# Attention and feed-forward on one core: the last unit's output in three PSUM places, and an order planned with another measure of TensorE's load

## The chip, the cores and the metric

The kernel runs on one core of one Trainium2 chip. The metric is the device time of one execution in microseconds (us); lower is better. The time before is the median of three runs. A profiled execution of the same kernel, taken apart from those three, gives the rows that are read here; its own time and its span stand in the table below. A difference of 0.3% is about what a measurement of this kernel can tell from none.

## What is computed

```python
# q, k, v: (4 batches, 8 heads, 768, 64); centroids (8, 16, 64); w_in (512, 2048); w_out (2048, 512)
q_assign = argmax(q_n @ c_n.T); k_assign = argmax(k_n @ c_n.T)      # nearest of 16 centroids, per head
mask = q_assign[:, :, :, None] == k_assign[:, :, None, :]
scores = where(mask, q @ k.T / sqrt(64), -1e9)
attn = exp(scores - max); attn = attn / (attn.sum(-1) + 1e-9)
x = (attn @ v).transpose(0, 2, 1, 3).reshape(3072, 512)
h = x @ w_in
g = where(h >= 1, h, where(h <= -1, 0, (h + 1)**2 / 4))
out = g @ w_out                                                       # (3072, 512) float32
```

All data are float32.

## The kernel before

**Tiling.** The work is cut into 12 units: four batches times three chunks of 256 queries (`u = b * NCH + c`). A unit goes through four head pairs, and each head pair through four tiles of 128 queries by 768 keys (`at_scores`, `at_soft`, `at_av`), and then through eight feed-forward steps `f` of 256 hidden columns (`ffn1`, `ffn2`). Float32 operands are split into two float16 parts, so that a product is three matmuls. Unit 0 is an exception: its operands are not split yet, and it works with float32 matmuls and turns the attention tiles with TensorE (`by_tensor`), where later units turn them by DMA.

**One tile of unit 0.** TensorE makes the scores (matmuls with 64 rows of the array in use, into `pair0` or `pair1`), VectorE reduces them (`tensor_tensor_reduce`, shown as CUSTOM_DVE_ANT_0 in the profile and as ISA in the order; it writes `sS`), ScalarE takes the exponential of `sS` in place, TensorE turns `sS` in six 128x128 pieces with the identity `idf`, and ScalarE copies them out to `pT`. After four tiles `at_av_first` multiplies `pT` with `v` into `bank_a`. Unit 0 has 16 such tiles, two in flight. Beside this, VectorE and ScalarE prepare the weights (`w_bits`: three passes of VectorE over 128x1024 numbers for each of 16 blocks, in `wk` and `w`), TensorE sums each block (`w_sum`, the product `wk,ones`), and the splits of `k` and `v` are made (`n<-kv,sc`, `kv<-kv,sv`).

**PSUM.** There are eight banks: `pair[0]` and `pair[1]` (two each, L562), `bank_a`, and `bankh`, `banki`, `bankj` (L563). Scores go to `pair0` after the first units, attention products to `bank_a`, hidden layers to the last three. `ffn2` (L1343) sums a unit's output, two tiles of 128x512, in `pair[1]`: at the first step it takes the place, at the last step ScalarE copies each tile with the factor `io` to the buffer `o`, and SyncE's queue sends it to memory.

**The last step of the last unit** differs by the flag `end`: the twelve products come tile by tile, one group for each tile, there are two copies by ScalarE, and two DMAs of 256 KB.

**What sets the order.** No instruction is issued where it is written. `Recorder` (L78) records all, and `issue` (L341) plans the order of every engine with a model of the chip: `price` (L126) gives each operation a cost, `Machine` (L358) follows engines, PSUM banks, the DMA queue and TensorE's clock, `forward` picks the next instruction by priority, and `backward` makes priorities from the plan just made. That is done `BASE` times; then each seed in `NUDGES` shifts the priorities of some recorded steps a little (`nudge`, L327), and a last `forward` gives the order that is written out. Products within one `with rec.group()` stay together.

**The clock in the model.** `Machine.product` (L404) cuts time in windows of `WINDOW` ns. In each it adds up the time in which TensorE works. If that is over `SLOW` of the window (`FULL`, when the clock was low), the next window is at full clock, and otherwise at half.

Of the kernel before, what the change touches and what calls it, by code (L numbers as in the profile page):

```python
# [35 lines left out]
WINDOW, SLOW, FULL = 3413.0, 0.41, 0.77  # L36
# [12 lines left out]
BASE = 5  # L49
NUDGES = (  # L50
# [27 lines left out]
class Recorder:  # L78
# [47 lines left out]
    def price(self, eng, op, out, ins, kw):  # L126
# [13 lines left out]
        if eng == "tensor":  # L140
            n = self.free(ins[1])
            half = self.free(ins[0]) <= 64 and n > 100
            if ins[1].dtype == F32:
                turn = kw.get("is_transpose", False)
                return 109 if turn else max(n / 1.2 + 2.5, 107) if half else max(n / 0.6 + 3, 222)

            return n / 4.8 + 3 if half else max(n / 2.4 + 2.5, 24)
# [25 lines left out]
    def add(self, eng, op, fn, args, kw):  # L173
# [10 lines left out]
        assert node.eng == eng  # L184
        p = self.price(eng, op, outs[0], ins, kw)
        if isinstance(p, tuple):
            node.cost += p[0]
            node.dma = p[1:]
        else:
            node.cost += p  # L190
# [167 lines left out]
class Machine:  # L358
# [20 lines left out]
    def run(self, x, t):  # L379
# [13 lines left out]
        else:  # L393
            x.busy = self.product(t, x.cost) if e == "tensor" else t + x.cost
# [9 lines left out]
    def product(self, t, cost):  # L404

        while True:
# [5 lines left out]
            t, self.work, cost = t + part, self.work + part, cost - part / pace  # L412
# [4 lines left out]
class Node:  # L417
    def __init__(self, eng, step, i):
        self.eng, self.step, self.i, self.ev = eng, step, i, 0
        self.banks = set()  # L420
        self.turn = False
        self.cost, self.dma, self.calls, self.preds, self.succs = 0.0, None, [], {}, []
# [52 lines left out]
def tile_clustered_attention_moe(  # L475
# [867 lines left out]
    def ffn2(u, f):  # L1343
# [4 lines left out]
        g = F.pop((u, f))  # L1348
        if e["first"]:
            F[u] = view(pair[1], [CT, DM], F32)  # L1350
        po = F[u]
        terms = [(s, i, *x) for s in range(2) for i, x in enumerate(((0, 0), (0, 1), (1, 0)))]
        end = u == NU - 1 and f == NF - 1

        parts = [(terms, [t]) for t in range(CT)] if end else [(terms[:3], range(CT)), (terms[3:], range(CT))]
        for part, ts in parts:
            with rec.group():
                for s, i, ga, wa in part:
                    for t in ts:
# [19 lines left out]
        if f == NF - 1:  # L1379
            to = out.rearrange("(b p t) e -> b p t e", b=B, t=T)[b, :, c * CT : (c + 1) * CT, :]  # L1380
            for part in [slice(t, t + 1) for t in range(CT)] if end else [slice(0, CT)]:
                rec.sync.dma_start(to[:, part], ob[:, part])


# [117 lines left out]
```

## Time and profile before

| what | us |
|---|---|
| median of 3 runs (lowest, highest) | 848.51 (847.31, 849.62) |
| the profiled execution's own time | 849.15 |
| its span, first to last instruction | 847.4 |
| TensorE busy in the span | 835.1 |
| VectorE, ScalarE, GpSimd busy | 624.5, 643.4, 445.4 |
| mean granted TensorE clock | 0.997 |

The profiled execution took 1.75 us more than its span (849.15 less 847.4) and 0.64 us more than the median. In the rows, PE is TensorE's matmuls, PEld its weight loads, DVE VectorE, ACT ScalarE, POOL GpSimd and SP SyncE, whose queue issues all DMAs. A row of the timeline has the start, the length, the engine, the operation, the tiles (written <- read) and the count; in brackets stands the idle time of the engine ahead of it and what ended it. Almost every instruction is issued from one line of the recorder (L355), so that rows are told apart by tiles. PEclk is the TensorE clock that was granted, as a share of the full one.

### The profile page before, as it was taken

What the parts mean: (1) busy time and instruction counts of PE and PEld (TensorE: products, weight loads), DVE (VectorE), ACT (ScalarE), POOL (GpSimd) and SP (SyncE); (2) the same over time, 40 slices, a digit from 0 to 9 for tenths busy, and PEclk for the clock granted to TensorE, in tenths of its full rate; (3) what the DMA queues carried; (4) which work ended last, traced back from release to release, by engine and by line L of the source; (5) the groups of instructions that cost most, each with busy time, mean ns of one, the idle gap of its engine ahead of it and who ended that gap; (6) DMA issues with size and microseconds to landing.
All of it is one profiled execution on the core that took longest, in us unless ns stands there. A gap on an engine that the chain in (4) does not pass through costs nothing.

```text
span 847.4 us, 22063 instructions
## 1 busy us (share of the span) xinstructions
PE 835.1 (99%) x8767; PEld 595.1 (70%) x8767; DVE 624.5 (74%) x1405; ACT 643.4 (76%) x1129; POOL 445.4 (53%) x365
## 2 busy tenths in 40 slices
PE   8998999999999999999999999999999999999997
PEld 6765667676777777776777677776777777777764
DVE  4999999899988767677878767678877767545222
ACT  5899867899979789687777887787778687766222
POOL 2001464456657567466555666565666656555221
PEclk9999999999999999999999999999999999999999
DMA  9929998999999879799999879898999887566100
GB/s 330 322 90 216 197 239 172 197 173 197 188 180 191 154 152 180 162 182 188 196 166 193 160 154 179 158 200 177 184 184 170 144 163 129 111 124 104 20 26 25
DMA packets 405415, 141.46 MB, mean 167 GB/s; under 512 B 373952, under 2 KB 397504, under 8 KB 405312
## 3 DMA queue, kind: packets, MB, share of 16 engines
q1 hardware_dynamic: 405312, 140.05, 82.6%
q8 instruction: 68, 1.11, 0.5%
q14 instruction: 35, 0.29, 0.1%
HBM read 40.40 MB, written 6.29 MB: 55 GB/s over the span
## 4 chain that ended last, share of the span: by engine, by line
PE 90%; DVE 6%; issue 1%; ACT 1%; DMA 1%; POOL 0%; SPq 0%; ACTq 0%; DVEq 0%
PE pair L355 45%; PE banka L355 12%; PE bankj L355 11%; PE banki L355 11%; PE bankh L355 11%; DVE w L355 1%; DVE sS L355 1%; DMA q<-in_q_dram 1%; ACT sS L355 1%; DVE bankj L355 0%; DVE r L355 0%; DVE wk L355 0%; DVE n L355 0%; DVE kv L355 0%; DVE banki L355 0%
## 5 line engine op out<-in xcount | busy, mean ns | idle before, releaser
L355 POOL TENSOR_TENSOR hl<-sS,hl 128x768 f16<-128x768 f32 x176 | 297.9, 1697 | 170.4 <-ACT hl L355 123.3
L355 PE MATMUL pair<-w,g 128*128 128x512 f16 (+1 forms) x1120 | 279.3, 391 | 0.0
L355 ACT ACTIVATE sS<-sS,sbi 128x768 f32<-128x768 f32 x192 | 179.1, 933 | 81.4 <-DVE sbi L355 69.4
L355 DVE CUSTOM_DVE_ANT_0 sS<-pair,zero,er 128x768 f32<-128x768 f32 x192 | 194.1, 1012 | 51.3 <-PE pair L355 42.1
L355 PEld LDWEIGHTS <-w 128*128 128x128 f16 x1848 | 179.3, 98 | 33.5 <-issue 0.9
L355 PEld LDWEIGHTS <-g 128*128 128x128 f16 x1056 | 101.9, 98 | 102.0
L355 PE MATMUL pair<-kv,q 128*128 128x384 f16 (+1 forms) x768 | 167.8, 341 | 0.4 <-DVE sbi L355 0.4
L355 ACT CAST hl<-sS 128x768 f16<-128x768 f32 x176 | 144.8, 826 | 12.3 <-DMA pT<-hl 10.0
L355 POOL TENSOR_TENSOR g<-r,g 128x512 f16<-128x512 f32 x80 | 95.0, 1188 | 90.3 <-ACT g L355 81.1
L355 PEld LDWEIGHTS <-q 128*128 128x128 f16 x1056 | 75.9, 97 | 43.9 <-issue 4.8
L355 PEld LDWEIGHTS <-pT 128*128 128x128 f16 x3168 | 98.3, 98 | 6.2 <-issue 1.1
L355 PE MATMUL banka<-kv,pT 128*128 128x64 f16 x3168 | 99.6, 193 | 0.0
L355 ACT ACTIVATE r<-r,f_ra,f_rs 128x512 f32<-128x512 f32 x80 | 64.7, 809 | 35.8 <-DVE r L355 35.3
L355 ACT CAST g<-r 128x512 f16<-128x512 f32 x80 | 48.8, 610 | 14.2 <-DVE r L355 9.6
L355 PE MATMUL bankj<-x,w 128*128 128x256 f16 (+1 forms) x368 | 47.8, 282 | 0.1
L355 POOL TENSOR_TENSOR qn<-qn,phi 128x256 f16<-128x256 f16 x44 | 29.4, 690 | 31.2 <-DVE phi L355 22.6
L355 PE MATMUL bankh<-x,w 128*128 128x256 f16 (+1 forms) x320 | 42.4, 284 | 0.4 <-DVE r L355 0.4
L355 PE MATMUL banki<-x,w 128*128 128x256 f16 (+1 forms) x280 | 41.2, 298 | 0.0
L355 ACT ACTIVATION_READ_ACCUMULATOR sS<-sS,sbi 128x1 f32 x192 | 36.0, 188 | 0.0
L355 POOL CAST rr<-rs 128x4 f16<-128x4 f32 x4 | 1.9, 471 | 60.8 <-DVE rs L355 43.8
L355 DVE TENSOR_SCALAR r<-banki,f_lo,f_hi 128x512 f32<-128x512 f32 x27 | 21.8, 806 | 15.7 <-PE banki L355 10.5
L355 DVE TENSOR_TENSOR rb<-banka,rs 128x256 f32<-128x256 f32 x44 | 18.5, 420 | 19.9 <-PE banka L355 19.5
(267 smaller groups left out, 1143.3 us busy)
## 6 DMA issues: line engine op xcount, KB each, us to landing
w<-in_moe_w_out_dram SPq DMA_DIRECT2D x14, 512.0 KB, 5.4
kv<-in_k_dram SPq DMA_DIRECT2D x16, 384.0 KB, 4.6
q<-in_q_dram SPq DMA_DIRECT2D x12, 512.0 KB, 5.1
kv<-in_v_dram SPq DMA_DIRECT2D x16, 384.0 KB, 4.3
out_dram<-o SPq DMA_DIRECT2D x11, 512.0 KB, 3.6
w<-in_moe_w_in_dram SPq DMA_DIRECT2D x10, 512.0 KB, 8.9
word<-in_moe_w_in_dram SPq DMA_DIRECT2D x6, 512.0 KB, 5.3
o<-in_v_dram SPq DMA_DIRECT2D x8, 384.0 KB, 4.6
```

Source lines behind the costliest of these rows:

```text
L355: fn(*args, **kw)
```

## The change

It has two parts.

**The last unit.** `ffn2` hands the last unit to a new function, `ffn2_last`. It sums the output in three places: tile 0 in `pair0` (512 columns), the left half of tile 1 in `pair1` and its right half in `bank_a` (256 columns each). In steps 0 to 6 the three places stand side by side in each group; in the last step each place has a group of its own, one after the other. Then ScalarE copies place 0, VectorE place 1, and place 2 is copied by ScalarE (128 columns) and VectorE (128 columns). Two DMAs of 256 KB follow, one for each tile. For a step of the last unit there are 18 matmuls in place of 12: six of 512 columns become twelve of 256.

**The planner.** A new number, `load`, is kept for each recorded step: the time in which columns stream through the array, without the fixed time of each instruction, and counted half where the products use 64 rows or fewer. `Machine.product` adds up this load in place of the time at work. The limits are 0.367 and 0.7 in place of 0.41 and 0.77, `BASE` is 4 in place of 5, and there are 153 new seeds in place of 116.

```diff
-WINDOW, SLOW, FULL = 3413.0, 0.41, 0.77
+WINDOW, SLOW, FULL = 3413.3, 0.367, 0.7
...
-BASE = 5
+BASE = 4
 NUDGES = (
-    1942955373, 816938251, 357356202, 374281491, 1996901420, 1807131614, 1896407074, 546410407, 980899077,
...
+    2072586604, 595665893, 1371912370, 1242582630, 2050099710, 1720864319, 412320839, 382347784, 317351908,
...
-                return 109 if turn else max(n / 1.2 + 2.5, 107) if half else max(n / 0.6 + 3, 222)
+                ns = 109 if turn else max(n / 1.2 + 2.5, 107) if half else max(n / 0.6 + 3, 222)
+                self.open.load += min(ns, n / (1.2 if half or turn else 0.6)) * (1 if ins[1].shape[0] > 64 else 0.5)
+                return ns
+            self.open.load += n / (4.8 if half else 2.4) * (1 if ins[1].shape[0] > 64 else 0.5)
...
-            x.busy = self.product(t, x.cost) if e == "tensor" else t + x.cost
+            x.busy = self.product(t, x.cost, x.load / x.cost) if e == "tensor" else t + x.cost
...
-            t, self.work, cost = t + part, self.work + part, cost - part / pace
+            t, self.work, cost = t + part, self.work + part * load, cost - part / pace
...
+        if u == NU - 1:
+            return ffn2_last(f, g, e)
...
+    def ffn2_last(f, g, e):
+
+        q = DM // 2
+        places = ((0, 0, pair[0][:, :DM]), (1, 0, pair[1][:, :q]), (1, q, bank_a[:, :q]))
+        terms = [(s, i, *x) for s in range(2) for i, x in enumerate(((0, 0), (0, 1), (1, 0)))]
+        for part, ps in [(terms, [x]) for x in places] if e["last"] else [(terms[:3], places), (terms[3:], places)]:
+            with rec.group():
+                for s, i, ga, wa in part:
+                    for t, c0, po in ps:
+                        rec.tensor.matmul(
+                            po, g[:, ga, s * CQ + t * P : s * CQ + (t + 1) * P],
+                            w2[f][:, wa, s, c0 : c0 + po.shape[1]],
+                            start=(e["first"] and s == 0 and i == 0), stop=(e["last"] and s == 1 and i == 2),
+                        )
...
+        rec.scalar.activation(out=ob[:, 0], in_=p0, func=AF.Copy, scale=e["io"])
+        rec.sync.dma_start(to[:, 0], ob[:, 0])
+        rec.vector.tensor_scalar(out=ob[:, 1, :q], in0=p1, scalar1=e["io"], scalar2=None, op0=ALU.mult)
+        rec.scalar.activation(out=ob[:, 1, q : q + P], in_=p2[:, :P], func=AF.Copy, scale=e["io"])
+        rec.vector.tensor_scalar(out=ob[:, 1, q + P :], in0=p2[:, P:], scalar1=e["io"], scalar2=None, op0=ALU.mult)
+        rec.sync.dma_start(to[:, 1], ob[:, 1])
```

**Where the rows move: the turns of unit 0.** The first place is TensorE's order at the fourth head pair of unit 0 (`kv_64`; the third is `kv_63`). `pair_82` and `pair_83` are `pair0` and `pair1`, `sS_88` to `sS_90` the three buffers of reduced scores, `hl_80` and `hl_81` the 0/1 labels, `banka` is `bank_a`. Before, the turns of the last two tiles stand right behind the scores of these tiles:

```order
L355 LDWEIGHTS hl_80
L355 MATMUL pair_83<-hl_81,hl_80 128x384
L355 MATMUL pair_82<-idf,sS_88 128x128 x6
L355 MATMUL pair_83<-idf,sS_89 128x128 x6
L355 LDWEIGHTS q_66
```

Now the third head pair's product with `v` (24 matmuls, of which the last two are shown) stands ahead of these turns:

```order
L366 MATMUL banka<-pT_146,kv_63 64x256
L366 MATMUL banka<-pT_147,kv_63 64x256
L366 MATMUL pair_82<-idf,sS_88 128x128 x6
L366 MATMUL pair_83<-idf,sS_89 128x128 x6
L366 LDWEIGHTS ones
```

What moved is the product with `v`: before, it stood two tiles earlier, between the scores and the turns of the first two tiles of that head pair. There TensorE's order now has nothing between the two:

```order
L366 LDWEIGHTS hl_80
L366 MATMUL pair_83<-hl_81,hl_80 128x384
L366 MATMUL pair_82<-idf,sS_89 128x128 x6
L366 LDWEIGHTS ones
L366 MATMUL banki<-wk_69,ones 128x128
```

A sum of weights (`wk,ones`, eight matmuls) now parts the two turns there.

**VectorE ahead of the third reduction of that head pair.** `w_72` and `word_71` are raw and prepared weights, `sS_88,sbi_137` is the reduction of the third tile. Before, between the reductions of the second and the third tile:

```order
L355 SCALAR_TENSOR_TENSOR w_72<-w_72 128x1024
L355 TENSOR_REDUCE zm_134<-bankj 128x16
L355 TENSOR_SCALAR wk_69<-wk_69 128x1024
L355 SCALAR_TENSOR_TENSOR kv_62<-kv_62,sv_168 128x768
L355 SCALAR_TENSOR_TENSOR w_72<-w_72,wk_69 128x1024
L355 RECIPROCAL sc_158<-ik_153 128x1
L355 TENSOR_TENSOR er_133<-bankj,zm_134 128x16
L355 SCALAR_TENSOR_TENSOR w_72<-w_72 128x1024
L355 ISA sS_88,sbi_137<-pair_82,zero,er_132 128x768
```

Now:

```order
L366 TENSOR_TENSOR zs_131<-banki,mx_129 128x256
L366 SCALAR_TENSOR_TENSOR w_72<-w_72,wk_69 128x1024
L366 TENSOR_SCALAR qn_67<-zs_131 128x16x16
L366 SCALAR_TENSOR_TENSOR w_72<-w_72 128x1024
L366 TENSOR_TENSOR bankj<-zs_131,has_130 128x256
L366 SCALAR_TENSOR_TENSOR w_72<-word_71 128x1024
L366 ISA sS_88,sbi_137<-pair_82,zero,er_132 128x768
```

Three passes over weights stand there in both; one is of another block now, and the split of `kv_62` has moved ahead of the first tile's reduction.

**The end of the program.** The second part of the change is seen on ScalarE and VectorE, with the engines that each instruction waits for (`g_77` is the last step's g, `o_68` the output buffer, `hl_79` the last step's hidden layer). ScalarE before:

```order
L355 CAST g_76<-hl_81 128x512 [waits DVE_49,PE_49,Pool_49]
L355 ACTIVATE hl_79<-hl_79,f_ra_185,f_rs_188 128x512 [waits DVE_49]
L355 CAST g_77<-hl_79 128x512 [waits DVE_49,PE_49,Pool_49]
L355 ACTIVATE o_68<-pair_83,f_io_182 128x512 [waits DMAHW2_49,PE_49]
L355 ACTIVATE o_68<-pair_83,f_io_182 128x512
```

ScalarE now:

```order
L366 CAST g_76<-hl_81 128x512 [waits DVE_49,PE_49,Pool_49]
L366 ACTIVATE hl_79<-hl_79,f_ra_185,f_rs_188 128x512 [waits DVE_49]
L366 CAST g_77<-hl_79 128x512 [waits DVE_49,PE_49,Pool_49]
L366 ACTIVATE o_68<-pair_82,f_io_182 128x512 [waits DMAHW2_49,PE_49]
L366 ACTIVATE o_68<-banka,f_io_182 128x128 [waits PE_49]
```

VectorE now (before, its last instruction was the one on `hl_79`):

```order
L366 SCALAR_TENSOR_TENSOR hl_81<-banki,f_gs_191,hl_81 128x512 [waits Activation_49]
L366 TENSOR_SCALAR hl_79<-bankj,f_lo_179,f_hi_176 128x512 [waits PE_49,Pool_49]
L366 SCALAR_TENSOR_TENSOR hl_79<-bankj,f_gs_191,hl_79 128x512 [waits Activation_49]
L366 TENSOR_SCALAR o_68<-pair_83,f_io_182 128x256 [waits DMAHW2_49,PE_49]
L366 TENSOR_SCALAR o_68<-banka,f_io_182 128x128 [waits Activation_49]
```

Two copies of 512 columns by ScalarE have become one of 512 and one of 128 columns, and VectorE has one of 256 and one of 128. Before, only the first of the two copies had a wait, and it was for TensorE's last product, since the products of both tiles raise TensorE's semaphore once, behind the last of them. Now each place raises it behind its own last product. VectorE's copy of 128 columns waits for ScalarE's. On SyncE's queue the first of the two last DMAs waits for ScalarE as before, and the second for VectorE in place of ScalarE.

More of the change, by code (lines that the diff above doesn't have):

```diff
@@ L184, in add @@
         assert node.eng == eng
+        kept, self.open = self.open, node
         p = self.price(eng, op, outs[0], ins, kw)
+        self.open = kept
         if isinstance(p, tuple):
@@ L402, in run, with product @@
         return end
-    def product(self, t, cost):
+    def product(self, t, cost, load):
         while True:
@@ L421, in __init__ @@
         self.turn = False
+        self.load = 0.0
         self.cost, self.dma, self.calls, self.preds, self.succs = 0.0, None, [], {}, []
@@ L1352, in ffn2 @@
         terms = [(s, i, *x) for s in range(2) for i, x in enumerate(((0, 0), (0, 1), (1, 0)))]
-        end = u == NU - 1 and f == NF - 1
-        parts = [(terms, [t]) for t in range(CT)] if end else [(terms[:3], range(CT)), (terms[3:], range(CT))]
-        for part, ts in parts:
+        for part in (terms[:3], terms[3:]):
             with rec.group():
                 for s, i, ga, wa in part:
-                    for t in ts:
+                    for t in range(CT):
                         rec.tensor.matmul(
@@ L1380, in ffn2 @@
             to = out.rearrange("(b p t) e -> b p t e", b=B, t=T)[b, :, c * CT : (c + 1) * CT, :]
-            for part in [slice(t, t + 1) for t in range(CT)] if end else [slice(0, CT)]:
-                rec.sync.dma_start(to[:, part], ob[:, part])
+            rec.sync.dma_start(to, ob)
+    def ffn2_last(f, g, e):
[11 more added lines that the diff above has]
+                        )
+        if not e["last"]:
+            return
+        ob = new("o", [CT, DM], F32)
+        to = out.rearrange("(b p t) e -> b p t e", b=B, t=T)[B - 1, :, (NCH - 1) * CT :, :]
+        (_, _, p0), (_, _, p1), (_, _, p2) = places
+        rec.scalar.activation(out=ob[:, 0], in_=p0, func=AF.Copy, scale=e["io"])
[4 more added lines that the diff above has]
+        rec.sync.dma_start(to[:, 1], ob[:, 1])
     ev = {}
```

30 rows, old and new, of the table NUDGES are left out of this document.

## Prediction

> **What bounds the kernel now.** I read the page first, then the table of stages, then the list of what TensorE waited for, and last the two places where it does not work: a spell near 82 us and the end.
>
> ```profile
> span 847.4 us, 22063 instructions
> PE 835.1 (99%) x8767; PEld 595.1 (70%) x8767; DVE 624.5 (74%) x1405; ACT 643.4 (76%) x1129; POOL 445.4 (53%) x365
> ```
>
> TensorE is busy for 835.1 of 847.4 us, so 12.3 us are all that it does not work. The stages say where they lie. The columns are the busy time of PE, PEld, DVE, ACT and POOL, then the granted clock, the DMA share and GB/s.
>
> ```profile
> 0.00:40.00 40.00, 36.75 (x334) 27.72 (x335) 27.54 (x70) 27.31 (x40) 7.06 (x35) 1.00 0.95 329
> 40.00:80.00 40.00, 38.07 (x311) 24.60 (x310) 39.42 (x94) 38.19 (x71) 4.59 (x10) 1.00 0.56 147
> 80.00:120.00 40.00, 38.52 (x279) 27.69 (x278) 38.74 (x67) 33.01 (x59) 18.30 (x13) 0.96 0.99 224
> 120.00:160.00 40.00, 40.00 (x391) 27.62 (x390) 36.77 (x82) 30.06 (x52) 22.10 (x15) 1.00 0.94 194
> 800.00:840.00 40.00, 40.00 (x274) 26.62 (x272) 12.49 (x16) 12.61 (x18) 9.49 (x9) 1.00 0.04 14
> 840.00:847.40 7.40, 2.58 (x12) 0.98 (x10) 0.00 (x0) 1.27 (x2) 0.00 (x0) 0.86 0.19 71
> ```
>
> Three stages lose time: 3.25 us before 40, 1.93 us to 80 and 1.48 us to 120. The end loses 4.82. From 40 to 120 VectorE is busy for 78.2 of 80 us, so there TensorE waits for what VectorE delivers late. After that TensorE is the bound, and no order of its work helps: the same products have to be done.
>
> ```profile
> PE pair L355 <- ACT sS L355: 3.7, 6, 1.3
> PE pair L355 <- DMA q<-in_q_dram: 1.0, 1, 1.0
> ```
>
> Of the idle time 3.7 us are six waits of the turns of unit 0 (`pair <- sS`) for ScalarE's exponential; the longest is 1.3. The other row is the start of the program, which stands in the same order in both kernels.
>
> The rest of what an order can save is the clock: it was 0.96 between 80 and 120. Narrower windows find the place, and the rows there its cause.
>
> ```profile
> 80.70:84.10 3.40, 2.01 (x11) 1.01 (x9) 3.40 (x7) 2.41 (x6) 0.00 (x0) 1.00 1.02 253
> 84.10:87.50 3.40, 3.38 (x18) 2.64 (x19) 2.48 (x5) 3.24 (x5) 0.69 (x2) 0.50 1.07 324
> ...
> 79.86 1.21 DVE L355 SCALAR_TENSOR_TENSOR w<-w 128x1024 uint32<-128x1024 uint32 x1
> 80.06 1.45 PE L355 MATMUL pair<-kv,q 64*128 64x384 f32 x4
> 81.00 1.00 DVE L355 CUSTOM_DVE_ANT_0 sS<-pair,zero,er 128x768 f32<-128x768 f32 x1
> 81.35 0.49 PE L355 MATMUL pair<-hl,hl 64*128 64x384 bf16 x2
> 82.04 0.94 ACT L355 ACTIVATE sS<-sS,sbi 128x768 f32<-128x768 f32 x1 [0.99 <-DVE sbi L355]
> 83.12 0.64 PEld L355 LDWEIGHTS pair<-idf,sS 128*128 128x128 f32 x6 [1.68 <-ACT sS L355]
> 83.12 2.54 PE L355 MATMUL pair<-idf,sS 128*128 128x128 f32 x12 [1.29 <-ACT sS L355]
> ```
>
> The window from 84.1 to 87.5 ran at half clock, and the one ahead of it holds the longest wait. VectorE was in a weight pass until 81.0, although the third tile's scores were written by about 80.1, when the fourth's begin; the reduction ended at 82.0, the exponential at 83.0, and TensorE stood for 1.29 us.
>
> **The change part by part.**
>
> *The half-clock window.* TensorE was at work for 2.01 of 3.40 us there, or 59%, over the old limit of 41%, so the old plan saw no slow window. By the new measure it had (0.65 + 0.49) / 2 us of products on 64 rows and 0.64 us of turns: 1.21 of 3.41 us, or 35%, under the new limit of 36.7%. So the new measure knows this window, and the old one did not. A window at half clock that is filled (3.38 of 3.40) does half of its work: it costs 1.7 us. In the new order the third head pair's product with `v` stands in the wait of 1.29 us. Its length:
>
> ```profile
> 73.38 0.41 PE L355 MATMUL banka<-idu,rr 128*64 128x128 f16 x8
> 73.63 2.76 PE L355 MATMUL banka<-pT,kv 128*64 128x256 f32 x24
> 76.32 1.59 PE L355 MATMUL pair<-idf,sS 128*128 128x128 f32 x12
> 77.79 0.62 PE L355 MATMUL banki<-wk,ones 128*128 128x128 bf16 x8
> 82.92 1.01 DVE L355 SCALAR_TENSOR_TENSOR n<-kv,sc,n 128x768 f16<-128x768 f32 x1
> ```
>
> From 73.38 to 76.32 it fills 2.94 us, more than the wait, so this window is no longer idle: **-1.7 us**, between -1.7 and 0 (another window may fall under the limit).
>
> A rule of the Trainium skill speaks against this term: "TensorE: Matmul & The Clock Gate", Part 1 on the HAM clock gate, has the clock fall to half after an idle window of about 3.4 us. The trace disagrees: a window with 59% of work was followed by half clock, so a wait of 1.3 us was enough. By the page's rule the order would not matter for the clock, and the term would be 0.
>
> *The waits of unit 0.* Where the product stood before, behind the scores of the head pair's first two tiles, the turns now follow at once. A reduction (1.00) and an exponential (0.94) lie between the end of a tile's scores and its turn, and the next tile's scores (1.45 + 0.49) cover them just if VectorE is free. If it is 0.9 us late, as at 81.0, that is 0.9 us of idle time; the second turn comes behind a reduction and an exponential more, with a turn (0.64) and a weight sum (0.62) to cover them, so up to 0.7 more. I take 0.9 of 0 to 1.6. Gone are the 1.29 us, so this makes -0.4.
>
> The other estimate is VectorE's queue, which has hardly any slack (78.2 of 80 us). Counted over both orders, it has ahead of unit 0's last reduction one split of `k` (1.01), one weight pass (1.21) and a maximum more, and four small ones less, so about 1.6 us more. TensorE has one more weight sum to do by then (0.62). If nothing else gives, TensorE idles for 1.0 us more; if VectorE's own idle time shrinks as much (it idled for 1.8 us between 40 and 120), for none. I take **-0.2 us**, between the two estimates, and for the range -2.0 (half of the 3.7 goes) to +1.5.
>
> SyncE's queue is reordered too, between the loads of `q`, `v` and weights. In the trace TensorE waited for a DMA at the start alone, so I cost that at nothing; without VectorE's backlog as cover, a late load would be one of the waits above.
>
> *The split products.* Twelve of 512 columns and 24 of 256 follow one another at the end:
>
> ```profile
> 816.40 2.75 PE L355 MATMUL pair<-w,g 128*128 128x512 f16 x12
> 818.99 2.78 PE L355 MATMUL bankj<-w 128*128 128x256 f16 x24
> 821.61 2.75 PE L355 MATMUL pair<-w,g 128*128 128x512 f16 x12
> ```
>
> Twelve take 818.99 - 816.40 = 2.59 us, or 215.8 ns each; 24 take 2.62 us, or 109.2 each. Two halves cost 2.5 ns more than a whole: times six per step, times eight steps, **+0.1 us**. Weight loads double with them, but those of the 256-column rows are hidden already. The new places add no wait: the last unit's first products need `x`, which comes after the last use of `pair0` and `bank_a`.
>
> *The end.* Here the last product ends at 842.58:
>
> ```profile
> 835.73 6.85 PE L355 MATMUL pair<-w,g 128*128 128x512 f16 x31
> ...
> 842.62 1.27 ACT L355 ACTIVATE o<-pair,f_io 128x512 f32<-128x512 f32 x2 [4.52 <-PE pair L355]
> 843.34 0.91 SPq L355 DMA_DIRECT2D out_dram<-o  x2
> ...
> 843.91 0.33 SPq L355 DMA_DIRECT2D out_dram<-o  x1
> ...
> L355 ACT ACTIVATE o<-pair,f_io 128x512 f32<-128x512 f32 x22 | 14.0, 679 | 5.4 <-PE pair L355 5.4
> L355 ACT CAST cT<-banki 128x128 f16<-128x128 f32 x1 | 0.3, 271 | 0.0
> ...
> L355 DVE TENSOR_SCALAR hl<-bankj,f_lo,f_hi 128x512 f32<-128x512 f32 x3 | 2.4, 810 | 5.7 <-PE bankj L355 5.7
> L355 DVE COPY cf<-banki 128x128 f32<-128x128 f32 x1 | 0.3, 291 | 0.7 <-PE banki L355 0.7
> ```
>
> Both copies came after the last product, and the second DMA was issued at 843.91, or 1.33 us behind it. Now place 0 is done twelve products of 256 columns earlier (1.31 us), so its copy (0.68) and its DMA lie beside products, and VectorE's copy of place 1 mostly too. Behind the last product stand ScalarE's copy of 128 columns, and then VectorE's, which waits for it. Each lies between the 128-column row (0.27, 0.29) and the 512-column row (0.68, 0.81) of its engine; I take 0.35, near the small ones, since the size is theirs. With 0.1 for three hand-overs (0.04 from product to copy in the trace) that is 0.8 us in place of 1.33: **-0.5 us**, between -0.7 and +0.25 (0.68 + 0.81 + 0.1). The 3.5 us from the second DMA's issue to the end stay.
>
> *The sum.* The profiled execution took 849.15 us, 1.75 more than its span and 0.64 more than the median. 849.15 - 1.7 - 0.2 + 0.1 - 0.5 = 846.85, or **846.9 us**. That is 1.6 us, or 0.19%, under the median of 848.51. The three runs lie 2.3 us apart, a little more than one half-clock window, so the slow ones may have had it and the fastest not; a kernel without it would have its median at the sum.
>
> **The rivals.**
>
> *A half-clock window stays (848.6 us).* For it: scores of unit 0 count half, so a window of 2.4 us of scores (1.2) and 1.0 us of idle time has 35%. The new place behind the first two tiles' scores has just this form, and idle time of about 1 us there decides. Against it: the plan was made with this limit. It gives the sum without the first term. This is also the case in which the second part doesn't do what it says, because the chip's clock goes by something else. The skill's page adds that the window is free-running, so that executions would cut the same order differently; no trace of a single execution shows that.
>
> *The waits shrink as well (845.1 us).* Half of the 3.7 us may go: the product of 2.94 us now covers the longest wait, and a plan that knows the clock can spread the cover. With -2.0 in place of -0.2 the sum is 845.05.
>
> *VectorE's backlog ends on the other side (851.5 us).* If the 1.6 us of added passes ahead of unit 0's last reduction come through, TensorE's turns wait 1.0 us longer at several tiles, each behind scores that count half, so that two windows run at half clock in place of one: 849.15 + 1.7 + 1.0 + 0.1 - 0.5 = 851.45. It decides from a second wait of about 1 us in a window of its own. Against it: the passes were moved, not added, and VectorE idles a little already.
>
> **How the numbers follow.** The forecast gets 0.46 (its own range is 845.6 to 848.1), the window that stays 0.25, the shrunken waits 0.22, the backlog 0.07. About 0.3% is what a measurement of this kernel can tell from no change: faster is below 845.96, slower above 851.06. Faster takes nearly all of the shrunken waits (0.21) and the lower part of the forecast (0.12): 0.33. Slower takes most of the backlog and a slip of the window that stays: 0.07. The same gets 0.60. The range is 844.2 to 849.4: from 0.9 below the shrunken waits (0.2 for the end's lower bound, 0.7 for more of the waits) to 0.8 above the window that stays (0.75 for the end's upper bound).
>
> **What would show it.** PEclk is 1.00 from 5 us to the end of TensorE's work; a window of 0.50 anywhere speaks for the first rival. The waits of `pair` for `sS` sum to 3.5 us or so, with none of 1.3 near 82 us and one of about 0.9 ahead of it. TensorE stays at 40.00 of 40 from 120 to 840. The last DMA is issued 0.8 us after the last product. The prediction is wrong if the waits grow past 5 us, if new ones stand behind 120 us, or if VectorE's last copy takes as long as one of 512 columns.

## The result, and the profile after

The changed kernel takes **852.62 us** (median of 20 executions, 849.84 to 861.53), the kernel before 848.94 (20 beside them, 846.94 to 858.4). The ratio is **1.0059, with a 95% interval of 1.0038 to 1.0079**: slower by 0.6%, or 5.0 us by the ratio (the two medians lie 3.7 us apart), where 846.9 us, no measurable change, was forecast, in a range of 844.2 to 849.4. The profiled execution took 851.88 us, with a span of 850.0.

The first lines of the page after:

```profile
span 850.0 us, 22156 instructions
PE 836.2 (98%) x8815; PEld 598.4 (70%) x8815; DVE 634.5 (75%) x1407; ACT 643.4 (76%) x1129; POOL 449.6 (53%) x365
```

TensorE's busy time grew by 1.1 us, the span by 2.6; VectorE's busy time grew by 10.0 us (624.5 before), of which its two new copies are 0.8. The stages of the changed kernel, and behind the dots the two long stages of the kernel before (PE, PEld, DVE, ACT, POOL busy, the granted clock, DMA share, GB/s):

```profile
0.00:40.00 40.00, 35.88 (x328) 27.21 (x329) 28.26 (x72) 28.84 (x44) 6.23 (x35) 1.00 0.95 330
40.00:80.00 40.00, 38.17 (x289) 24.21 (x288) 39.83 (x89) 37.14 (x66) 7.53 (x10) 1.00 0.68 158
80.00:120.00 40.00, 39.34 (x304) 27.61 (x303) 38.43 (x69) 33.81 (x61) 18.25 (x12) 1.00 0.97 227
120.00:480.00 360.00, 356.83 (x3956) 255.60 (x3955) 299.13 (x669) 289.26 (x513) 216.56 (x159) 1.00 0.93 177
480.00:840.00 360.00, 359.86 (x3902) 259.83 (x3900) 227.28 (x511) 252.56 (x446) 199.63 (x149) 1.00 0.73 135
...
120.00:480.00 360.00, 359.60 (x3972) 257.54 (x3970) 294.60 (x685) 293.79 (x518) 217.49 (x160) 1.00 0.95 180
480.00:840.00 360.00, 359.60 (x3867) 256.54 (x3866) 224.23 (x495) 249.80 (x443) 197.99 (x149) 1.00 0.73 134
```

The half-clock window between 80 and 120 us is gone from this execution (1.00; 0.96 before). Up to 120 us TensorE idles for 6.61 us, as before (6.66); but 1.0 of the 6.66 is the wait for the first `q` load, which the profile after does not have. The larger loss stands behind 120 us, where TensorE was the bound: 3.31 us of idle time there in place of 0.80. What TensorE waited for in the changed kernel (us in total, times, longest):

```profile
PE pair L366 <- DVE sbi L366: 1.9, 3, 0.8
PE pair L366 <- ACT sS L366: 1.7, 4, 0.7
PE bankh L366 <- DVE er L366: 1.6, 1, 1.6
PE bankj L366 <- DVE wk L366: 0.9, 1, 0.9
PE banki L366 <- DVE wk L366: 0.9, 2, 0.5
PE bankh L366 <- DVE hl L366: 0.6, 1, 0.6
```

The turns' waits for ScalarE (`sS`) fell from 3.7 to 1.7 us, but waits for VectorE took their place: `wk`, `hl` and 0.8 of `sbi` in unit 0, the rest behind 120 us. The longest, for `er`, is at 227 us. TensorE, VectorE and GpSimd there:

```profile
225.00 1.48 PE L366 MATMUL bankj<-x,w 128*128 128x256 f16 x12
226.31 0.81 PE L366 MATMUL pair<-kv,q 128*128 128x384 f16 x4
228.69 0.75 PE L366 MATMUL bankh<-cT,kv 128*128 128x16 f16 x24 [1.56 <-DVE er L366]
...
225.00 1.05 DVE L366 SCALAR_TENSOR_TENSOR bankh<-ik,iq 128x1 f32<-128x1 f32 x1
226.08 1.63 DVE L366 TENSOR_TENSOR bankh<-zs,has 128x64 f32<-128x64 f32 x1
...
228.47 0.16 DVE L366 TENSOR_TENSOR er<-bankh,zm 128x4 f32<-128x4 f32 x1
...
224.87 1.16 POOL L366 TENSOR_TENSOR g<-r,g 128x512 f16<-128x512 f32 x1
225.99 1.64 POOL L366 TENSOR_TENSOR hl<-sS,hl 128x768 f16<-128x768 f32 x1
```

A step of one column takes 1.05 us and one of 64 columns 1.63. Both end just behind a GpSimd step: at 226.05 and 227.71, where those end at 226.03 and 227.63. They are held while GpSimd works (a run with GpSimd's steps made short bears this out, below). The groups of one such step, the first row of the kernel before, the second of the changed one:

```profile
L355 DVE TENSOR_SCALAR qn<-zs 128x256 f16<-128x256 f32 x8 | 2.3, 287 | 0.3
...
L366 DVE TENSOR_SCALAR qn<-zs 128x256 f16<-128x256 f32 x8 | 6.6, 824 | 0.2
```

The same eight steps take 4.3 us more. Summed over all steps of VectorE that last 0.15 us or more above the short ones of their form, the held time is about 25 us before and about 35 after. The Trainium skill, "SBUF — State Buffer", section "Who interferes with whom", has an exclusive port pair that VectorE's steps with two SBUF inputs, or in a 2-port mode, share with GpSimd; the later one waits for the whole instruction of the other. The rows above agree with it.

The end of the changed kernel:

```profile
844.87 0.69 ACT L366 ACTIVATE o<-pair,f_io 128x512 f32<-128x512 f32 x1 [3.26 <-PE pair L366]
845.33 0.82 PE L366 MATMUL banka<-w,g 128*128 128x256 f16 x6
845.53 0.48 DVE L366 TENSOR_SCALAR o<-pair,f_io 128x256 f32<-128x256 f32 x1 [4.64 <-PE pair L366]
...
846.18 0.37 ACT L366 ACTIVATE o<-banka,f_io 128x128 f32<-128x128 f32 x1 [0.62 <-PE banka L366]
846.59 0.35 DVE L366 TENSOR_SCALAR o<-banka,f_io 128x128 f32<-128x128 f32 x1 [0.57 <-ACT o L366]
```

The last products end at 846.15 (845.33 + 0.82), VectorE's last copy at 846.94, and the last DMA is issued at 846.96: 0.8 us behind the last product, as forecast. From the last product to the end of the span it is 3.85 us, where it was 4.82 before (847.4 - 842.58): 1.0 us less in place of the 0.5 forecast, since the stretch from the last issue to the end is 3.0 us here, where the forecast let 3.5 stay.

**The clock over many executions.** Five of the 20 executions took 859.66 to 861.53 us at a mean granted clock of 0.986 to 0.988. Nine had a clock of 0.999 or 1.0: a median of 850.35 us. Of 96 executions of the kernel before beside the experiments (two more, of 963 and 3058 us, are left out), 33 had that clock (median 847.46), and four lay at 0.989 or below (855.16 to 858.95). So the change costs 2.9 us at full clock, and the rest is a clock that drops more often or for longer. The mean of the 20 (853.97) lies 3.6 us above their median at full clock, the mean of the 96 (849.05) 1.6 above theirs: 2.0 us more. 2.9 + 2.0 = 4.9, beside the 5.0 of the ratio. At full clock too the nine executions spread over 2.9 us (849.84 to 852.73), so that a median of a few of them is good to a microsecond or so.

### The profile page after: what moved, and what is told of

It reads as the page before. It is cut to its first block, busy times and chain, and to the rows that moved or that the text cites. A ratio compares the mean times of both kernels' runs of the same rounds, so it can differ in the third digit from the quotient of the medians.

```text
span 850.0 us, 22156 instructions
## 1 busy us (share of the span) xinstructions
PE 836.2 (98%) x8815; PEld 598.4 (70%) x8815; DVE 634.5 (75%) x1407; ACT 643.4 (76%) x1129; POOL 449.6 (53%) x365
## 5 line engine op out<-in xcount | busy, mean ns | idle before, releaser
L366 PE MATMUL pair<-w,g 128*128 128x512 f16 (+2 forms) x1120 | 278.3, 387 | 0.0
L366 PEld LDWEIGHTS <-g 128*128 128x128 f16 x1104 | 106.2, 98 | 98.6
L366 POOL TENSOR_TENSOR g<-r,g 128x512 f16<-128x512 f32 x80 | 97.0, 1212 | 86.0 <-ACT g L366 77.7
L366 ACT ACTIVATE q<-q,phi 128x512 f16<-128x512 f16 x44 | 31.0, 718 | 7.1 <-DVE phi L366 5.3
L366 DVE TENSOR_SCALAR r<-bankh,f_lo,f_hi 128x512 f32<-128x512 f32 x27 | 21.8, 807 | 15.9 <-PE bankh L366 13.8
```

The source lines that it names most:

```text
L366: fn(*args, **kw)
```

## The experiments

The table has all of them, with the clock of 0.999 or 1.0 called full. Each ratio is to the kernel before on the same chip. Two single executions, of 4883 us (three_places_alone) and 1449 us (new_to_120_then_old), are left out.

| run | median us | median at full clock (of n) | clock under 0.99 | ratio (95%) |
|---|---|---|---|---|
| three_places_alone | 847.97 | 846.84 (5 of 12) | 1 | 0.9982 (0.9955, 1.0009) |
| new_plan_alone | 856.59 | 851.13 (2 of 12) | 6 | 1.0079 (1.0044, 1.0114) |
| old_to_120_then_new | 860.61 | none (of 6) | 2 | 1.0139 (1.0083, 1.0194) |
| new_to_120_then_old | 851.73 | 849.77 (3 of 11) | 2 | 1.0037 (1.0005, 1.0069) |
| four_waits_covered | 852.58 | 852.58 (5 of 5) | 0 | 1.0053 (1.0041, 1.0065) |
| three_places_two_waits_covered | 848.54 | 848.42 (5 of 12) | 1 | 1.0003 (0.9967, 1.0038) |
| held_steps_moved | 851.67 | 851.43 (6 of 12) | 2 | 1.0042 (1.0014, 1.007) |
| three_places_held_steps_moved | 846.83 | 845.5 (6 of 12) | 1 | 0.9977 (0.9953, 1.0002) |
| new_order_gpsimd_quarter | 848.57 | 846.67 (5 of 12) | 4 | 1.0015 (0.9989, 1.004) |
| old_order_gpsimd_quarter | 845.1 | 844.96 (3 of 6) | 0 | 0.9962 (0.9949, 0.9974) |
| three_places_av_moved | 855.69 | none (of 6) | 0 | 1.0092 (1.0068, 1.0115) |
| three_places_weight_pass_moved | 848.87 | 848.26 (4 of 13) | 2 | 0.9989 (0.9968, 1.001) |
| early_wait_covered | 851.72 | 851.37 (1 of 6) | 0 | 1.0044 (1.0032, 1.0056) |
| held_steps_and_early_wait | 850.34 | 850.0 (8 of 12) | 0 | 1.0013 (0.999, 1.0035) |
| no_seeds_old_measure | 861.17 | none (of 6) | 2 | 1.0131 (1.0106, 1.0157) |
| no_seeds_new_measure | 860.68 | 856.1 (1 of 6) | 1 | 1.013 (1.0103, 1.0156) |

### The two parts, each alone

The order of before with the three places:

```diff
-WINDOW, SLOW, FULL = 3413.3, 0.367, 0.7
+WINDOW, SLOW, FULL = 3413.0, 0.41, 0.77
-BASE = 4
+BASE = 5
-    2072586604, 595665893, 1371912370, 1242582630, 2050099710, 1720864319, 412320839, 382347784, 317351908,
...
+    1942955373, 816938251, 357356202, 374281491, 1996901420, 1807131614, 1896407074, 546410407, 980899077,
...
-            t, self.work, cost = t + part, self.work + part * load, cost - part / pace
+            t, self.work, cost = t + part, self.work + part, cost - part / pace
```

> The order of before on every engine, with the last unit's three places added. Theory W (the new order brings waits behind 120 us, about 4 us of them; the three places themselves save about 0.8 us at the end): 0.6 to 1.0 us under before, ratio about 0.999, no new wait behind 120 us, the last DMA issued 0.8 us after the last product. Rival P (the three places cost TensorE time, by split products or by occupied banks): 1 to 4 us over before. Rival C (the new order falls into half clock more often): as theory W here.

The new plan with the old end:

```diff
-        if u == NU - 1:
-            return ffn2_last(f, g, e)
...
+        end = u == NU - 1 and f == NF - 1
...
```

> The order of the changed kernel, with the last unit as it was before. Theory W: 0.8 us over the changed kernel, so about 3.4 us over before by its profile (span near 851), ratio 1.005 to 1.008, with the same waits near 227, 266, 378 and 469 us. Rival P: about as before, ratio 1.000. Rival C: several of its executions near 860 us at a mean clock of 0.987, as in the changed kernel, and the others close to before.

The three places alone are 0.6 us faster at full clock (847.46 less 846.84), though the interval of their ratio reaches 1.0009. The new plan alone loses: 856.59 us. So the loss is the order's.

### Which part of the order

Two orders are spliced at 120 us of planned time, one the other way round:

```diff
...
+        (head, start), (tail, _) = (new, old) if HEAD_NEW else (old, new)
+        head = head[: next(i for i, x in enumerate(head) if start[x] > CUT)]
+        done = set(head)
+        self.order = head + [x for x in tail if x not in done]
```

> Three places; what the old plan starts in its first 120 us stands in the old order, and the rest in the new order. Theory W: the waits behind 120 us come with the new order, so 2 to 4 us over before, ratio 1.003 to 1.005. Rival B (VectorE's backlog in unit 0 is the loss): about 0.8 us under before. Rival C (the half clock comes from unit 0's stage in the new order): no more executions near 860 us than before has.

> Three places; what the new plan starts in its first 120 us stands in the new order, and the rest in the old order. Theory W: stage to 120 us about 0.5 us better than before, no more than 0.8 us of waits behind it, the end 0.8 us shorter: 1 us under before, ratio 0.998 to 1.000. Rival B: 1 to 3 us over before. Rival C: about one execution in four near 860 us, as in the changed kernel.

The old head with the new tail is the slowest of the four; the new head with the old tail is 3.8 us slower in the median than the old order with the three places. Both miss what theory W expected (2 to 4 us over the kernel before, and 1 us under it). A splice makes waits at its seam (2.1 us for `q<-qn` at 130 us in the first), so neither a size nor a half of the order that loses is taken from these two.

### Other products put into the waits

In the changed kernel, four groups of products go behind the group that follows; in the old order with the three places, two. The numbers are places in TensorE's order: the first goes behind the second. The loop that moves them is not shown:

```diff
+MOVES = ((212, 213), (250, 251), (357, 358), (448, 449))
...
```

> The changed kernel, with four groups of products moved behind the next group in TensorE's order, at the four largest waits behind 120 us (1.56, 0.49, 0.35 and 0.61 us; the order of the other engines stays). Theory W (these waits are time of the kernel): they go, with 0.16 us each that the row of a wait hides, so 3.0 + 0.66 = 3.7 us less: executions at full clock throughout at about 846.2 to 848 us in place of 849.8 to 852, median about 849 and ratio to before near 1.001. Rival (a wait only shifts: VectorE, late there, is late at the next product as well): the waits come back some us later, and time and ratio (1.006) stay.

```diff
+MOVES = ((406, 408), (563, 564))
...
```

> The order of before with the three places, and two groups of products moved behind the next ones where the kernel before waits behind 120 us (0.40 us each, at 423 and 584 us). Theory W: 0.8 + 0.33 = 1.1 us less than three_places_alone, so 844.4 to 846.3 at full clock, median 847.2, ratio to before 0.997. Rival (waits shift): as three_places_alone, 848.3 and 0.998.

Both rivals held: no gain, 852.58 and 848.54 us. TensorE's waits with the four groups moved:

```profile
PE pair L374 <- DVE sbi L374: 1.6, 2, 0.8
PE banki L374 <- DVE zm L374: 1.6, 1, 1.6
...
PE banki L374 <- DVE n L374: 0.7, 1, 0.7
...
PE bankh L374 <- DVE er L374: 0.3, 1, 0.3
```

The wait for `er` fell from 1.6 to 0.3 us, but others appear, for `zm` (1.6) and `n` (0.7). That fits a VectorE that is late, so that the next product finds it late.

### VectorE's held steps moved

Entries name the engine, the place moved and its target:

```diff
+MOVES = (("vector", 385, 380), ("vector", 386, 380), ("vector", 464, 466), ("vector", 765, 766))
...
```

> The changed kernel, with the order of VectorE alone changed at three places: two small steps of VectorE that were held while GpSimd worked (1.05 and 1.63 us in place of 0.2, at 225 us) go 4 us ahead, where GpSimd idles; at 265 and 467 us the reduction that TensorE waits for goes ahead of a held step (1.61 and 1.52 us). TensorE's order stays. Theory H (the new waits behind 120 us come from VectorE's steps that are held by GpSimd's, so they go when the held step is no longer ahead of what TensorE waits for): waits of 1.56, 0.49 and 0.60 us and 0.16 each behind the rows, 3.1 us in all, go: median 849.5, at full clock from 846.7, ratio 1.002. Rival (the waits only shift, as they did when TensorE's order was changed at these places): median 852.6, ratio 1.005, other waits of 2 to 3 us in sum behind 227 us.

```diff
+MOVES = (("vector", 695, 696), ("vector", 922, 921), ("vector", 923, 921))
...
```

> The order of before with the three places, and VectorE's order changed at the two places behind 120 us where the kernel before waits (0.40 us each): at 421 us the reduction goes ahead of the held step (0.99 us), at 580 us the held step (1.43 us) goes ahead of a step of 0.80 us, to where GpSimd idles. Theory H: 0.8 + 0.33 = 1.1 us less than three_places_alone: median 847.2, from 844.4 at full clock, ratio to before 0.997. Rival (shift): 848.3 and 0.998, other waits in place of these.

In the old order the theory held (846.83 us, 847.2 expected). TensorE's waits there:

```profile
PE pair L372 <- ACT sS L372: 3.7, 6, 1.3
PE bankh L372 <- POOL ones L600: 1.0, 1, 1.0
PE bankj L372 <- DVE wk L372: 0.4, 1, 0.4
PE pair L372 <- DMA kv<-in_k_dram: 0.4, 1, 0.4
PE bankj L372 <- DVE zs L372: 0.3, 1, 0.3
```

All of these lie in unit 0; behind 120 us none is left. It is the fastest version run that does the whole computation (0.9977, though its interval reaches 1.0002); at full clock it is 2.0 us under the kernel before. In the new order the rival held: at full clock 851.43, no gain. The three waits went or shrank, but others stand in their place, such as these two:

```profile
PE banki L378 <- DVE n L378: 0.6, 1, 0.6
PE banki L378 <- DMA q<-qn: 0.6, 1, 0.6
```

So two single waits could be mended here, and the moves at three places did not mend a VectorE that is held at many more.

### GpSimd made short

Both orders are kept on every engine; only GpSimd's subtractions shrink to a quarter of their columns, from the second write of each buffer on. The rest of what they should write is left out of the computation:

```diff
+                    if x.eng == "gpsimd" and out is not None and kw.get("op") == ALU.subtract:
+                        at = out.tensor.name
+                        if at in full:
+                            kw = {k: v[:, : v.shape[1] // 4] if k in ("out", "in0", "in1") else v for k, v in kw.items()}
+                        full.add(at)
```

> The changed kernel with its order on every engine kept, but GpSimd's subtractions (the low halves of the attention weights, of g and of the factors rs) work on a quarter of their columns; the rest of these low halves is left out of the computation. Theory H (GpSimd holds VectorE, VectorE is late, TensorE waits): VectorE's held time falls from 35 us to under 12, the waits behind 120 us from 3.3 us to under 1, and the time by about 3.9 to a median of 848.7, from 846 at full clock; the distance to old_order_gpsimd_quarter is 1.5 us, what unit 0 costs. Rival (VectorE's queue as such is ordered worse): waits and distance to the old order stay (4.3 us), whatever GpSimd does.

> The order of before with the three places, with the same cut of GpSimd's steps to a quarter (the same part is left out). Theory H: held time from 25 to under 10 us, the two waits of 0.40 us go, 1.1 us less than three_places_alone: median 847.2, from 844.4 at full clock. Rival: 848.3, or 4.3 us under new_order_gpsimd_quarter.

The busy times, the new order first:

```profile
PE 842.5 (99%) x8815; PEld 604.6 (71%) x8815; DVE 607.3 (71%) x1407; ACT 642.5 (75%) x1129; POOL 197.6 (23%) x365
...
PE 833.2 (99%) x8815; PEld 598.8 (71%) x8815; DVE 606.1 (72%) x1407; ACT 644.0 (76%) x1129; POOL 192.0 (23%) x365
```

VectorE's busy time is now the same in both orders (607.3 and 606.1), where 634.5 and 626.1 stood with GpSimd's full steps. The new order is 3.7 us faster at full clock than the changed kernel (846.67 against 850.35), the old one 1.9 (844.96 against 846.84; 1.1 was expected). Long GpSimd steps thus cost about 1.8 us more in the new order. The distance between the orders falls from 3.5 us to 1.7, where 1.5 was expected and 4.3 by the rival. These are medians of three to nine executions, so 1.8 and 1.7 are rough; and GpSimd's own results also come sooner here, which no run parts from the hold. Two waits behind 120 us are left in the new order (0.5 and 0.3 us), none in the old one. The new order also fell to a low clock in 4 of 12 executions, so that this part of the loss does not hang on GpSimd's steps.

### The waits of unit 0

The old order with the three places, once with the product with `v` moved into the wait of 1.29 us (`banka` behind the fourth tile's scores), once with one weight pass of VectorE moved behind the reduction:

```diff
+MOVES = ((76, 81),)
...
```

> The order of before with the three places, and the one move that the prediction speaks of: the third head pair's product with v goes behind the fourth tile's scores, into the wait of 1.29 us. The kernel to compare with is three_places_alone: median 848.3, at full clock throughout 845.6 to 847.4. The prediction's steps (window gone -1.7; 1.29 gone and 0.9 (0 to 1.6) new ahead of the turns where the product stood): no half-clock window between 80 and 95 us in any execution, so that more runs lie at full clock, a median of 846.8, and executions at full clock 0 to 0.4 us faster. Rival (unit 0 is bound by VectorE's queue, so what the move gains at one place comes back at the next): executions at full clock the same within 0.3 us or slower, and waits of 1.3 us in sum ahead of the two turns.

```diff
+MOVES = (("vector", 147, 148),)
...
```

> The order of before with the three places, and one weight pass of VectorE (1.21 us) moved from ahead of the third tile's reduction to behind it, at the wait of 1.29 us in unit 0. If this wait is the pass's (the prediction's reading): the wait falls to about 0.2 us, no half-clock window behind it, executions at full clock 1 us faster than three_places_alone (from 844.5), median 847.0. Rival (VectorE's queue as a whole bounds unit 0, so that the pass is late at the next turn): the wait comes back at the turns of the next tiles, median 848.3, but spread over two windows, so that the half-clock window may still go.

TensorE in the first of them, and behind the dots in the second:

```profile
72.59 0.88 PE L368 MATMUL pair<-idf,sS 128*128 128x128 f32 x6 [0.45 <-ACT sS L368]
75.67 1.54 PE L368 MATMUL pair<-idf,sS 128*128 128x128 f32 x6 [2.21 <-ACT sS L368]
...
91.26 0.88 PE L368 MATMUL pair<-idf,sS 128*128 128x128 f32 x6 [1.40 <-ACT sS L368]
...
92.27 0.87 PE L372 MATMUL pair<-idf,sS 128*128 128x128 f32 x6 [1.04 <-ACT sS L372]
94.34 1.54 PE L372 MATMUL pair<-idf,sS 128*128 128x128 f32 x6 [1.20 <-ACT sS L372]
```

In the old order of VectorE the move that the prediction costed is a loss: 0.45 + 2.21 us new where the product had stood, the old wait still 1.40, and half clock from 75.47 to 89.12, in all 855.69 us. The weight pass only splits the wait into 1.04 and 1.20 us. In the changed kernel, where VectorE's order is another one, the same product does fill the wait:

```profile
74.51 0.87 PE L366 MATMUL pair<-idf,sS 128*128 128x128 f32 x6 [0.68 <-ACT sS L366]
...
76.26 0.88 PE L366 MATMUL pair<-idf,sS 128*128 128x128 f32 x6 [0.25 <-ACT sS L366]
...
80.74 2.76 PE L366 MATMUL banka<-pT,kv 128*64 128x256 f32 x24
83.43 1.53 PE L366 MATMUL pair<-idf,sS 128*128 128x128 f32 x12
```

The turns at 83.43 follow the product without a gap, and where it had stood before, the new waits are 0.68 + 0.25 = 0.93 us. So the move is good or bad by what VectorE does beside it. That a wait in unit 0 moves along VectorE's queue (busy for 39.83 of 40 us from 40 to 80) fits all three, and is argued.

### The long spell at half clock

The early wait alone is covered (the turn of the labels at 16 us goes behind the next six products), and then together with the held steps:

```diff
+MOVES = ((20, 21),)
...
```

> The changed kernel with one swap at 16 us: the turn of the labels (eight products, bankh from idf,hl), which waits 0.63 us for VectorE, goes behind the next six products (bankj from cf,kv), as it stood before the change. Theory C (the long half-clock spell of unit 0 starts when a window of the clock begins at about 15 to 16 us, where this wait makes the load low): runs over 857 us, 5 of 20 with the changed kernel, become 0 or 1 in 12; the median goes from 852.6 to about 851.3. Rival (the spell can start in any of the many low windows up to 35 us): 3 or more of 12 stay over 857. Theory W alone expects 0.3 us less and nothing else.

```diff
+MOVES = (("tensor", 20, 21), ("vector", 385, 380), ("vector", 386, 380), ("vector", 464, 466), ("vector", 765, 766))
...
```

> The changed kernel with the moves of held_steps_moved and the swap of early_wait_covered together. If the loss of the change is the waits behind 120 us (theory H) and the long half-clock spell from the early wait (theory C), nothing of it is left but what the new order of unit 0 costs at full clock: median 849.0, from 846.4, no run over 857. If H fails: median 851.7 as with the swap alone.

What the spell looks like in new_plan_alone, in windows of its clock:

```profile
15.49:18.90 3.41, 2.78 (x25) 2.45 (x24) 3.26 (x9) 2.86 (x3) 0.00 (x0) 1.00 1.11 347
18.90:22.32 3.42, 3.42 (x8) 1.69 (x7) 2.24 (x6) 0.69 (x2) 0.00 (x0) 0.50 1.04 387
22.32:39.38 17.06, 16.58 (x95) 12.62 (x94) 9.29 (x21) 8.39 (x15) 0.00 (x0) 0.50 0.66 224
```

A window with the early wait (0.63 us) is followed by six at half clock. With the new order up to there, 19 of 72 executions had a clock under 0.99; with the old one, 11 of 163; with the new one and the swap, 0 of 18. Where a window begins matters: in the profiles of the new order the spell came where one began at 15.44, 15.49 or 16.20 us (at 16.20 for two windows only), and full clock stayed where one began at 14.79, 16.42 or 16.90. The old order has the spell in two profiles, with a window from 15.21 and from 15.23, and not with one from 15.83 or 16.02. So the early wait makes the spell more frequent, and is not its only start. The swap does what was expected for the spell (its rival needed 3 of 12), and its median is 851.72, where 851.3 was expected. Together with the held steps it is 850.34, not the 849.0 expected; other waits stand behind 120 us here too.

### The measure or the seeds

Both planners without any seed, with the three places and four rounds of priorities; the first also has the old limits and the old way to add up:

```diff
-    2072586604, 595665893, 1371912370, 1242582630, 2050099710, 1720864319, 412320839, 382347784, 317351908,
...
+NUDGES = ()
```

> The three places, the planner with the old measure of load and old limits (4 rounds of priorities), no seeds: the order as the plan makes it before any search. Beside no_seeds_new_measure it tells what the measure alone does. Both should be slower than before, by 3 to 10 us. Theory M (the new measure itself makes orders that wait more): this one is the faster of the two by 2 us or more. Rival S (the measure is neutral, and what the change lost lies in its set of seeds, found for a planner that does not know that GpSimd holds VectorE): the two within 1.5 us.

> As no_seeds_old_measure, with the new measure of load and the new limits. Theory M: 2 us or more slower than that. Rival S: within 1.5 us of it. If the new measure does what it is made for: fewer half-clock windows in unit 0 than with the old measure, so the faster of the two by 1.7 us or more.

861.17 and 860.68 us: no difference that six executions of each, spread over 13 and 7 us, can show, and the clock drops with both. The old set of seeds, with its fifth round of priorities, is worth 13.2 us (861.17 less 847.97), the new one 8.1 (860.68 less 852.62). So in time, what the change lost lies in what its seeds gain. The held time is another matter: without any seed VectorE is busy for 645.9 us by the new measure and 638.2 by the old one, so that more of it comes with the new measure alone.

Why the new order is worse stays open. The reason given above, a planner that does not know of the hold, does not fit the code: in both kernels `turns` (L161 in the kernel before) marks GpSimd's steps (but `memset`), and VectorE's with two operands in SBUF or a copy or `tensor_scalar` from SBUF to SBUF. `Machine` lets such a step begin at the earliest 185 ns (VectorE) or 118 ns (GpSimd) before the end of the one that holds the port (`TURN`, `port`). That the steps on the chip fall out of the planned times, and are then held where the plan has room, is a guess that no run tests.

## Why the prediction was wrong, step by step

- **"After that TensorE is the bound, and no order of its work helps"**, said of the time behind 120 us, is the step that failed. It holds for TensorE's own products, and it was used as if nothing there could get worse either. A new order also places VectorE's steps anew against GpSimd's. The windows show 2.5 us more of idle time there (3.31 less 0.80); with 0.17 us that the row of each wait hides (below), and five waits more, 3.4. The sum had no term for it, although the last part of the prediction named new waits behind 120 us as what would prove it wrong.
- **The half-clock window, -1.7.** It is gone in the profile after, but the term took one execution for all. A third of the executions of before (33 of 96) are at full clock and cannot have paid for such a window. The version with the held steps moved in the old order has the same wait and keeps full clock:

```profile
80.87:84.29 3.42, 2.02 (x15) 1.59 (x16) 3.42 (x7) 3.22 (x7) 0.00 (x0) 1.00 0.97 314
84.29:87.70 3.41, 2.98 (x35) 1.86 (x35) 3.41 (x8) 3.38 (x6) 0.69 (x2) 1.00 1.21 266
```

  TensorE worked for 59% of the first window, as much as in the one ahead of the half clock before, and the next is at 1.00. The Trainium skill ("TensorE: Matmul & The Clock Gate", Part 1) has windows that run free of the kernel, which the prediction set aside for want of a trace; these runs agree with it. The first rival was nearer: half clock stays, elsewhere and far longer, for 2.0 us more in the mean.
- **The waits of unit 0, -0.2.** At the turns the first estimate came out: the product with `v` fills the wait of 1.29 us, and 0.93 us are new where 0.9 was taken; the waits for `sS` fall by 2.0 us in all. What was missed is that VectorE is then late elsewhere: new waits for `wk` (1.8), `sbi` (0.8) and `hl` (0.6). That the idle time up to 120 us is the same in sum (6.61 for 6.66) is luck. The profile before holds the 1.0 us for the first `q` load, which no other profile of the old order has; without it TensorE idles for 0.9 us more. That is the other estimate, VectorE's queue (1.0), and the range of the term holds it.
- **The split products and the end, +0.1 and -0.5.** The last issue comes 0.8 us behind the last product, as worked out. The end as a whole gave 1.0 us in this profile, more than the 0.7 of its range, by what follows the last issue. The three places alone gain about 0.6 us at full clock; no run has the split products by themselves.
- **The rival of VectorE's backlog (851.5)** had the right sign and engine. Its 1.0 us of more idle time in unit 0 is there, at other products than the turns; its two half-clock windows did not come there, and it had nothing behind 120 us, where most of the loss stands.
- **The sum with what was measured**, at full clock: -0.6 for the three places, about +1.8 for the long GpSimd steps, about +1.7 for the rest of the order, 2.9 in all. With 2.0 for the clock it is 4.9. What the 1.7 consists of is not shown. Two waits behind 120 us (0.5 and 0.3 us) are part of it, and unit 0 may be: up to 120 us TensorE idles for 6.61 us in the changed kernel and for 5.98 in the old order with the held steps moved, whose profile is at full clock too.

## What to carry to other kernels

Where one engine is busy all the time, a new order of the others can still lose time: cost what they may be late with, and not only what TensorE has to do. If a step of few columns takes far longer than the shortest of its group, look for the GpSimd step that ends with it before anything is moved on the engine that waits. A clock window seen in one profile belongs to one execution: take its share over many before it becomes a term.

## What was not expected of the hardware

- **GpSimd holds VectorE.** Steps of 0.16 to 0.3 us took up to 1.63 us. The kernel's planner has a rule for it, and the prediction had no term. With a quarter of GpSimd's columns, and no step of its own changed, VectorE's busy time fell by 27 us (634.5 to 607.3).
- **Half clock can stay.** Once down at 18.9 us, where products use 64 rows, the clock stays down for six windows, although TensorE has work for 16.58 of 17.06 us. This costs about 10 us; in the profile of the changed kernel, where full clock holds past 19 us, the same products keep it.
- **A wait costs 0.17 us more than its row says.** The row of twelve products at 225.00 lasts 1.48 us, but the next products start 1.31 us after it: the last 0.17 us of a row lie under the next row, if there is nothing to wait for. Ahead of a wait they don't.
